# A convolution by spectra with a soft mixture of experts: a new order inside a step, and the filter's spectrum loaded two steps ahead

## The chip, the cores and the metric

The kernel runs on one core of one Trainium2 chip. The metric is device time in microseconds of one execution; lower is better. Engines are named as the profile does: PE (TensorE), with its weight loads as PEld, DVE (VectorE), ACT (ScalarE), POOL (GpSimd) and SP (SyncE, which here only issues transfers).

## What is computed

```python
def _attn_ref(x, h):                      # x (8, 5696, 128), h (5696, 128), float32
    B, S, D = x.shape
    L = 2 * S
    Xf = np.fft.rfft(x, n=L, axis=1)
    Hf = np.fft.rfft(h, n=L, axis=0)
    return np.fft.irfft(Xf * Hf[None], n=L, axis=1)[:, :S, :]

def _moe_ref(x, phi, w1, w2):             # x: the (45568, 128) rows of the above
    logits = x @ phi                      # 32 slots, 8 experts
    d = np.exp(logits - logits.max(0, keepdims=True))
    d /= d.sum(0, keepdims=True) + 1e-09
    slot_input = (d.T @ x).reshape(E, S_per_e, D)
    for e in range(E):
        slot_out[e] = np.maximum(slot_input[e] @ w1[e], 0.0) @ w2[e]
    c = np.exp(logits - logits.max(1, keepdims=True))
    c /= c.sum(1, keepdims=True) + 1e-09
    return c @ slot_out.reshape(n_slots, D)
```

A long convolution of 8 sequences with one filter, then a softmax over tokens (down each column of the logits) that gathers 32 slots, a small two-layer network on them, and a softmax over slots (along each row) that spreads them back.

## The kernel before

Both transforms of the convolution are products with constant tables on PE. The length is split as 90 x 64. The filter `h` goes first as block 0, then the 8 sequences; each block is 8 chunks. A loop over t = 0 to 79 (line 598) is a software pipeline written out by hand: every engine runs its instructions in the order in which the code records them. In one step:

- `stage_a` (t < 72): 128 small products of the folded input `xf` with the table `s1` (L245), in four tiles ("banks") of PSUM, each copied to `ft` by ACT (L251). `next_x` then folds the next input on POOL (L230) and issues loads.
- `stage_b1` (from t = 8, twice a step): forward products into `bt` (L285), then DVE multiplies them with the filter's spectrum `ht` (L309) and combines them into `yf` (L319). `ht` is made in steps 8 to 15, stored to `h_spec`, and from then on loaded a chunk at a time (`load_h`, L272); there are two `ht` buffers and two of each `yf`.
- `stage_b2`, one step later: backward products of `yf` (L335), copied by ACT to `zst` (L340) and stored to the tensor `z` (L343).
- From t = 26 on the rest works on a "pair" of chunks, spread over several steps. `pair(lag)` is the number of the pair whose turn is `lag` steps after its first; pairs start in even steps. `stage_c1` (even, lag 0) turns `z`, loaded to `zc`, into tokens `y`: two pairs of products (L388), folds on DVE (L393, L394), then four folds on POOL (L407). `stage_c2` (odd, lag 1) transposes `y` in four tiles (L416), copied by ACT to `yt` (L418). `stage_c3` (odd) gives the logits (L425), copied to `lt` (L428). `column_max` takes the running maximum of each column on DVE (L436, L441, L444). `stage_c4` (even, lag 2) transposes the logits (L454), takes the exponent of the column softmax into `dt` on ACT (L460) and the maximum of each row on DVE (L469), subtracted on POOL (L470). `stage_c5` (even) transposes `dt` (L477) into `d`. `softmax` finishes the row softmax: Exp on ACT (L485), token sums on DVE (L487 to L489), product on POOL (L490). `dispatch` multiplies `d` with `y` on PE (L501), and DVE adds the result to `acc` (L506). `stage_c6` (odd, lag 5) transposes the row softmax (L525) and stores it.

All PSUM tiles but `bt` come from one ring of four banks (`bank()`). A tile that gets a bank again waits until the engine that reads the last tile in it has done so: `yt`, `zst` and `ft` copies by ACT, the c1 folds and the addition to `acc` by DVE.

Steps 72 to 79 have no `stage_a`. After the loop come the stages of the last pairs, the network on the slots, and the product that writes the output.

Of the kernel before, what the change touches and what calls it, by code (L numbers as in the profile page):

```python
# [10 lines left out]
F32 = mybir.dt.float32  # L11
# [63 lines left out]
def kernel(  # L75
# [25 lines left out]
    P = 128  # L101
    B, S, D = x.shape
    NSL = moe_phi.shape[1]
    E, _, F = moe_w1.shape
# [5 lines left out]
    NJ = HALF // CH  # L110
    NU = (NP + 1) // 2
    KG = 2 * ((NU + NJ - 1) // NJ)
# [48 lines left out]
    bpool = front.enter_context(tc.tile_pool(name="bpool", bufs=1))  # L161
# [91 lines left out]
    prods, hs = {}, {}  # L253
# [8 lines left out]

    def spectrum(c):
        if c not in hs:
            hs[c] = bpool.tile([P, 2, KG * D], F32, name="ht", tag="ht", bufs=2)
            if c == NJ - 1:
                nc.gpsimd.memset(hs[c][:, :, :], 0.0)
        return hs[c]

    def load_h(c):  # L270
        if NJ <= c < (B + 1) * NJ:
            nc.sync.dma_start(out=spectrum(c)[:, :, :], in_=hd[c % NJ])  # L272
# [4 lines left out]
    def stage_b1(u):  # L277
        g, j, part, us = parts(u)
        bt = bps.tile([P, 2, 2, 2 * D], F32, name="bt", tag=f"bt{part}")
        for o, (i, n) in enumerate(us):  # L280
            for a in range(2):
                r = slice(a * HP, (a + 1) * HP)
                for q in range(n):
                    f_ = 2 * ((2 * i + q) % KG)
                    nc.tensor.matmul(bt[q * HP:(q + 1) * HP, a, o, :], wt[r, 2 * i + q, :],  # L285
                                     block(ft, g, r, j)[:, :, f_:f_ + 2, :].rearrange(
                                         "p s c d -> p c s d"),
                                     start=True, stop=True)
        m, r = len(us), slice(0, us[0][1] * HP)

        if m == 2:
            pv = bt[r, :, :, :].rearrange("p a o (c d) -> p (a o) c d", c=2)
        else:
            pv = bt[r, :, 0, :].rearrange("p a (c d) -> p a c d", c=2)
        k = 2 * m
        pi = bpool.tile([P, 4, 2, D], F32, name="p", tag="pi", bufs=1)
        ht = spectrum(u // 2)
        h0 = part * (KG - 2) * D
        hv = [ht[r, v, h0:h0 + k * D].rearrange("p (k d) -> p k d", d=D) for v in range(2)]
        for v, p_ in ((1, pi[r, 0:k, :, :]), (0, pv)):  # L300
            if g:
                h_ = hv[v]
            else:
                i = us[0][0]
                h_ = turn[r, v, :, i:i + m].unsqueeze(3).broadcast_to([r.stop, 2, m, D]) if m == 2 else \
                    turn[r, v, :, i].unsqueeze(2).broadcast_to([r.stop, k, D])
            if g or m == 1:
                h_ = h_.unsqueeze(2).broadcast_to([r.stop, k, 2, D])
                nc.vector.tensor_tensor(out=p_, in0=pv, in1=h_, op=AL.mult)  # L309
            else:  # L310
                for a in range(2):
                    nc.vector.tensor_tensor(
                        out=p_[:, 2 * a:2 * a + 2, :, :], in0=pv[:, 2 * a:2 * a + 2],
                        in1=h_[:, a].unsqueeze(2).broadcast_to([r.stop, m, 2, D]), op=AL.mult)
        if g:
            y_ = bpool.tile([P, 4 - 2 * part, 2, D], F32, name="yf", tag=f"yf{part}", bufs=2)
            prods[u] = y_
        for c, op_ in ((0, AL.subtract if g else AL.add), (1, AL.add if g else AL.subtract)):
            nc.vector.tensor_tensor(out=y_[r, 0:k, c, :] if g else hv[c], in0=pv[:, :, c, :],  # L319
                                    in1=pi[r, 0:k, 1 - c, :], op=op_)  # L320

    def stage_b2(u):
        g, j, part, us = parts(u)
        if g == 0:
            return
        m = len(us)
        y_ = prods.pop(u)
        n = us[0][1]
        st = bpool.tile([P, 2 - part, 2, 2 * D], F32, name="zst", tag=f"zst{part}", bufs=2 - part)
        bz = [bank() for _ in range(n)]  # L330
        for o, (i, _) in enumerate(us):
            for q in range(n):
                r = slice(q * HP, (q + 1) * HP)
                for a in range(2):
                    nc.tensor.matmul(bz[q][a * HP:(a + 1) * HP, o * 2 * D:(o + 1) * 2 * D],  # L335
                                     vt[r, i, a, :],
                                     y_[r, a * m + o, :, :].rearrange("p c d -> p (c d)"),
                                     start=True, stop=True)
        for q in range(n):
            nc.scalar.activation(st[:, 0:m, q, :],  # L340
                                 bz[q][:, 0:m * 2 * D].rearrange("p (o x) -> p o x", o=m), AF.Copy)
        k, q0 = m * n, 2 * us[0][0]
        nc.sync.dma_start(  # L343
            out=zd[g - 1][q0:q0 + k, :, :, :].rearrange("q r c d -> r q (c d)"),
            in_=st[:, :, :, :].rearrange("p o q x -> p (o q) x")[:, 0:k, :])
# [66 lines left out]
    def stage_c2(T):  # L412
        for k in (3, 1, 0, 2) if tail else (3, 2, 1, 0):
            p = bank()
            for i in range(CH):
                nc.tensor.transpose(p[:, i * TR:(i + 1) * TR], ys[T][0:TR, k * CH + i, 0:D],  # L416
                                    ident[0:TR, 0:TR])
            nc.scalar.activation(yt[:, k * CH:(k + 1) * CH, :, :], of_tokens(p), AF.Copy)  # L418
# [75 lines left out]
    def dispatch(T):  # L494
        ap_ = bank()
        d_ = ds.pop(T)
        y_ = ys.pop(T)
        for i in range(CH):
            for k in range(Q):
                r = slice(k * NSL, (k + 1) * NSL)  # L500
                nc.tensor.matmul(ap_[r, 0:D + 1], d_[:, i, r], y_[:, k * CH + i, :],  # L501
                                 start=(i == 0), stop=(i == CH - 1))
        if T == 0:
            nc.vector.tensor_copy(out=acc[:, :], in_=ap_[:, 0:D + 1])
        else:
            nc.vector.scalar_tensor_tensor(out=acc[:, :], in0=acc[:, :],  # L506
                                           scalar=scales.pop(T)[:, 0:1], in1=ap_[:, 0:D + 1],
                                           op0=AL.mult, op1=AL.add)
# [89 lines left out]
    for t in range(last_front + 1):  # L598
        us = [2 * (t - LAG_B) + k for k in range(2)] if t >= LAG_B else []

        def pair(lag):
            T, half = divmod(t - LAG_C - lag, 2)
            return T if half == 0 and 0 <= T < NT else None

        for u in us:
            stage_b1(u)
        if us:
            c = us[0] // 2
            if c < NJ:
                store_h(c)  # L610
            else:
                del hs[c]
            load_h(c + 1)
        for u in wait_b2:
            stage_b2(u)
        wait_b2 = us
        if t < NA:
            stage_a(t)
            next_x(t + NJ)
        if pair(3) is not None:  # L620
            dispatch(pair(3))
        T, U = pair(0), pair(2)
        if t == last_front:
            assert T is None and U is None
            stage_c2(pair(1))
            for u in us:
                stage_b2(u)
            wait_b2 = []
            V = pair(1)
            stage_c6(V - 2)  # L630
            stage_c3(V)
            column_max(V)
            break
        rows = (lambda: None) if U is None else (lambda: stage_c4(U))
        after = None
        if T is not None:
            after = stage_c1(T, rows)
        else:
            rows()
        if pair(1) is not None:  # L640
            stage_c2(pair(1))
        if pair(5) is not None:
            stage_c6(pair(5))
        if after:
            after()
        if pair(-2) is not None:
            load_pair(pair(-2))
        if U is not None:
            stage_c5(U)
        if pair(1) is not None:  # L650
            stage_c3(pair(1))
        if pair(1) is not None:
            column_max(pair(1))
        if U is not None:
            softmax(U)
        if t == NA:
            lead.close()
            wts = inner.enter_context(tc.tile_pool(name="wts", bufs=1, side="right"))
            w1s = wts.tile([P, E, F], F32, name="w1s")
        if NA <= t < NA + E:  # L660
            nc.sync.dma_start(out=w1s[:, t - NA, :], in_=moe_w1[t - NA])

    T = V + 1
    (_, n0, p0), (_, n1, p1) = z_blocks(N1)
# [213 lines left out]
```

## Time and profile before

| | |
|---|---|
| median of 3 runs | 973.12 us (970.54 to 976.52) |
| the profiled execution | 971.23 us, its span 969.1 us |
| PE, PEld busy | 778.9 us (80%), 524.8 us (54%) |
| DVE, ACT, POOL busy | 678.4 us (70%), 468.9 us (48%), 367.8 us (38%) |
| mean granted clock of PE | 0.92 |
| moved by DMA | 223.94 MB, mean 231 GB/s |

A row of a group or of the timeline names the line of the kernel, the engine, the operation, what it writes and reads, and the shapes; "idle before <-releaser" is the time the engine stood still just before, and what ended it. A row of the waits has the total in us, how many times, and the longest. "issue" as a releaser means that the profile shows nothing that the engine waited for. PEclk is the share of its full clock that PE was granted. Each float32 product stands as two matrix instructions.

### The profile page before, as it was taken

How to read it: one execution, taken by the hardware profiler on the slowest of the kernel's cores; microseconds unless marked ns; L12 is line 12 of the kernel's file. 1: busy time of each engine (PE TensorE's matmuls, PEld its weight loads, DVE VectorE, ACT ScalarE, POOL GpSimd, SP SyncE). 2: the span in 40 equal slices, each digit the busy share in tenths (PEclk: the TensorE clock that was granted, in tenths of full speed). 3: DMA queues.
4: the chain of work that ended last, by engine and by line, in shares of the span. 5: the costliest groups of instructions: out<-in, count | busy, mean ns of one | idle time of the engine just before them, and what ended most of it. 6: DMA issues, size and time to landing. Idle time of an engine off the chain costs nothing.

```text
span 969.1 us, 36172 instructions
## 1 busy us (share of the span) xinstructions
PE 778.9 (80%) x15860; PEld 524.8 (54%) x15860; DVE 678.4 (70%) x1117; ACT 468.9 (48%) x1040; POOL 367.8 (38%) x357
## 2 busy tenths in 40 slices
PE   2677678779879898888888988998978888786893
PEld 2655455545555565565555655655655443244783
DVE  5378677657758778687776777877868997673542
ACT  1432244335545565455555555555645454465442
POOL 1024333344444444445554554543314224463000
PEclk9999899979989999999998999999989998887955
DMA  9642678886757777686777776766748988853598
GB/s 220 208 130 114 209 228 261 284 256 219 240 182 253 236 239 234 207 260 217 230 232 229 231 236 221 233 213 210 223 162 287 307 287 223 240 187 125 223 405 339
DMA packets 95783, 223.94 MB, mean 231 GB/s; under 512 B 7382, under 2 KB 57046, under 8 KB 92485
## 3 DMA queue, kind: packets, MB, share of 16 engines
q1 hardware_dynamic: 95051, 221.29, 70.8%
q8 instruction: 124, 2.03, 0.9%
q10 hardware_dynamic: 576, 0.36, 0.2%
q14 instruction: 32, 0.26, 0.1%
HBM read 140.10 MB, written 81.42 MB: 229 GB/s over the span
## 4 chain that ended last, share of the span: by engine, by line
PE 49%; DMA 12%; DVE 11%; issue 6%; ACT 5%; POOL 3%; SPq 0%; DVEq 0%; ACTq 0%; POOLq 0%
PE bank L245 12%; PE bank L388 10%; PE bt L285 7%; PE bank L335 5%; PE bank L416 4%; DMA out_dram<-o 3%; DVE yf L319 3%; DMA zd<-z 3%; ACT zst L340 3%; PE bank L425 3%; DVE p L309 3%; DVE bt L309 2%; DMA z<-zst 2%; PE bank L501 2%; DMA cl<-c_t 2%
## 5 line engine op out<-in xcount | busy, mean ns | idle before, releaser
L245 PE MATMUL bank<-s,xf 128*32 128x90 f32 (+1 forms) x9216 | 210.5, 249 | 62.7 <-issue 25.2
L245 PEld LDWEIGHTS bank<-s,xf 128*32 128x32 f32 x9216 | 193.4, 138 | 96.2 <-ACT zst L340 41.6
L230 POOL TENSOR_TENSOR xf<-xc 128x512 f32<-128x512 f32 x100 | 125.5, 1276 | 253.2 <-PE bank L245 246.6
L251 ACT ACTIVATE ft<-bank 128x384 f32<-128x384 f32 x288 | 140.6, 492 | 116.3 <-PE bank L245 96.6
L340 ACT ACTIVATE zst<-bank 128x256 f32<-128x256 f32 (+1 forms) x248 | 100.4, 485 | 124.4 <-PE bank L335 107.6
L309 DVE TENSOR_TENSOR p<-bt,ht 128x512 f32<-128x512 f32 (+2 forms) x128 | 116.7, 912 | 35.7 <-DMA ht<-h_spec 26.4
L285 PE MATMUL bt<-ft,wt 64*64 64x256 f32 x1620 | 118.1, 408 | 27.5 <-DVE yf L319 13.3
L319 DVE TENSOR_TENSOR yf<-bt,p 128x256 f32<-128x256 f32 (+2 forms) x256 | 126.5, 535 | 4.4
L388 PE MATMUL bank<-zc,i 128*64 128x512 f32 x480 | 117.7, 613 | 4.1 <-DMA z<-zst 1.9
L309 DVE TENSOR_TENSOR bt<-bt,ht 128x512 f32<-128x512 f32 (+2 forms) x128 | 118.0, 922 | 0.0
L436 DVE TENSOR_REDUCE mx<-lt 64x1 f32<-64x360 f32 x64 | 33.1, 518 | 99.9 <-ACT lt L428 99.4
L335 PE MATMUL bank<-yf,vt 64*64 64x256 f32 x1440 | 98.5, 380 | 5.1 <-DVE om L394 3.6
L285 PEld LDWEIGHTS bt<-ft,wt 64*64 64x64 f32 x1620 | 58.5, 141 | 80.6 <-issue 44.0
L418 ACT ACTIVATE yt<-bank 128x360 f32<-128x360 f32 x128 | 54.9, 472 | 80.6 <-PE bank L416 80.6
L416 PE MATMUL bank<-ident,y 109*128 109x109 f32 x512 | 69.4, 290 | 24.6 <-DVE acc L506 10.8
L407 POOL TENSOR_TENSOR y<-y,op 128x512 f32<-128x512 f32 x64 | 77.5, 1210 | 9.9 <-DVE op L393 7.1
L416 PEld LDWEIGHTS bank<-ident,y 109*128 109x128 f32 x512 | 58.0, 159 | 35.6 <-issue 16.9
L335 PEld LDWEIGHTS bank<-yf,vt 64*64 64x64 f32 x1440 | 58.7, 134 | 31.3 <-DVE om L394 5.4
L407 POOL TENSOR_TENSOR y<-y,om 128x512 f32<-128x512 f32 x54 | 64.7, 1198 | 2.1
L462 POOL MEMSET dt<- 64x8 f32 x32 | 3.4, 107 | 145.7 <-issue 111.0
L501 PE MATMUL bank<-y,d 128*32 128x129 f32 x1024 | 38.7, 283 | 24.3 <-issue 21.0
L388 PEld LDWEIGHTS bank<-zc,i 128*64 128x64 f32 x480 | 29.9, 138 | 51.6 <-issue 43.7
(104 smaller groups left out, 899.1 us busy)
## 6 DMA issues: line engine op xcount, KB each, us to landing
ht<-h_spec SPq DMA_DIRECT2D x64, 768.0 KB
zc<-z SPq DMA_DIRECT2D x30, 1024.0 KB
z<-zst SPq DMA_DIRECT2D x56, 512.0 KB
xc<-in_x_dram SPq DMA_DIRECT2D x52, 320.0 KB
z<-zst SPq DMA_DIRECT2D x64, 256.0 KB
out_dram<-o SPq DMA_DIRECT2D x16, 1024.0 KB
zc<-z SPq DMA_DIRECT2D x30, 416.0 KB
h_spec<-ht SPq DMA_DIRECT2D x8, 768.0 KB
```

The source lines that it names most:

```text
L230: eng.tensor_tensor(out=to, in0=ab[0], in1=ab[1], op=AL.subtract if comp else AL.add)
L245: nc.tensor.matmul(p[r:r + HALF, k * W:k * W + w_], x_, s1[:, comp, a, 0:w_], start=True, stop=True)
L251: nc.scalar.activation(to, v, AF.Copy)
L285: nc.tensor.matmul(bt[q * HP:(q + 1) * HP, a, o, :], wt[r, 2 * i + q, :], block(ft, g, r, j)[:, :, f_:f_ + 2, :].rearrange("p s c d -> p c ...
L309: nc.vector.tensor_tensor(out=p_, in0=pv, in1=h_, op=AL.mult)
L319: nc.vector.tensor_tensor(out=y_[r, 0:k, c, :] if g else hv[c], in0=pv[:, :, c, :], in1=pi[r, 0:k, 1 - c, :], op=op_)
L335: nc.tensor.matmul(bz[q][a * HP:(a + 1) * HP, o * 2 * D:(o + 1) * 2 * D], vt[r, i, a, :], y_[r, a * m + o, :, :].rearrange("p c d -> p (c ...
L340: nc.scalar.activation(st[:, 0:m, q, :], bz[q][:, 0:m * 2 * D].rearrange("p (o x) -> p o x", o=m), AF.Copy)
L388: nc.tensor.matmul(p[h_ * HP:(h_ + 1) * HP, :], i1[0:kr, tab, :], t_[0:kr, h_, o, :, q, :], start=True, stop=True)
L407: eng.tensor_tensor(out=part_, in0=part(v, 0), in1=o_[:, :, :], op=sign)
L416: nc.tensor.transpose(p[:, i * TR:(i + 1) * TR], ys[T][0:TR, k * CH + i, 0:D], ident[0:TR, 0:TR])
L501: nc.tensor.matmul(ap_[r, 0:D + 1], d_[:, i, r], y_[:, k * CH + i, :], start=(i == 0), stop=(i == CH - 1))
```

## The change

It touches the `ht` and `yf` buffers and the order of the loop's body. `ht` gets a third buffer, and each `yf` loses one. The spectrum for step t + 2 is loaded in step t (in step 15 those for 16 and 17), behind the `z` stores on SP. The two halves of `stage_b1` and of the last step's `stage_b2` alternate. In an odd step `stage_c2` and `stage_c6` now precede `stage_a`. `dispatch` moves from the odd step with lag 3, behind `stage_a`, to the even step with lag 4, ahead of it. `column_max` moves from the end of the odd step to the next even step, behind `dispatch` and `stage_a` in the order of recording and ahead of `stage_c1`. `softmax` moves from the end of the even step to the end of the next odd one, behind `stage_c3`. The arithmetic and the number of instructions that compute are the same.

```diff
--- before.py
+++ after.py
@@ -262,7 +262,7 @@
 
     def spectrum(c):
         if c not in hs:
-            hs[c] = bpool.tile([P, 2, KG * D], F32, name="ht", tag="ht", bufs=2)
+            hs[c] = bpool.tile([P, 2, KG * D], F32, name="ht", tag="ht", bufs=3)
             if c == NJ - 1:
                 nc.gpsimd.memset(hs[c][:, :, :], 0.0)
         return hs[c]
@@ -313,7 +313,7 @@
                         out=p_[:, 2 * a:2 * a + 2, :, :], in0=pv[:, 2 * a:2 * a + 2],
                         in1=h_[:, a].unsqueeze(2).broadcast_to([r.stop, m, 2, D]), op=AL.mult)
         if g:
-            y_ = bpool.tile([P, 4 - 2 * part, 2, D], F32, name="yf", tag=f"yf{part}", bufs=2)
+            y_ = bpool.tile([P, 4 - 2 * part, 2, D], F32, name="yf", tag=f"yf{part}", bufs=1)
             prods[u] = y_
         for c, op_ in ((0, AL.subtract if g else AL.add), (1, AL.add if g else AL.subtract)):
             nc.vector.tensor_tensor(out=y_[r, 0:k, c, :] if g else hv[c], in0=pv[:, :, c, :],
@@ -602,65 +602,58 @@
             T, half = divmod(t - LAG_C - lag, 2)
             return T if half == 0 and 0 <= T < NT else None
 
-        for u in us:
-            stage_b1(u)
+        for k in range(2):
+            if us:
+                stage_b1(us[k])
+            if wait_b2:
+                stage_b2(wait_b2.pop(0))
         if us:
             c = us[0] // 2
             if c < NJ:
                 store_h(c)
             else:
                 del hs[c]
-            load_h(c + 1)
-        for u in wait_b2:
-            stage_b2(u)
+            for n in (c + 1, c + 2) if c == NJ - 1 else (c + 2,):
+                if c >= NJ - 1:
+                    load_h(n)
         wait_b2 = us
+        T, U, V = pair(0), pair(2), pair(1)
+        if V is not None:
+            stage_c2(V)
+            if t == last_front:
+                while wait_b2:
+                    stage_b2(wait_b2.pop(0))
+            if pair(5) is not None:
+                stage_c6(pair(5))
+        if pair(4) is not None:
+            dispatch(pair(4))
         if t < NA:
             stage_a(t)
             next_x(t + NJ)
-        if pair(3) is not None:
-            dispatch(pair(3))
-        T, U = pair(0), pair(2)
-        if t == last_front:
-            assert T is None and U is None
-            stage_c2(pair(1))
-            for u in us:
-                stage_b2(u)
-            wait_b2 = []
-            V = pair(1)
-            stage_c6(V - 2)
-            stage_c3(V)
-            column_max(V)
-            break
-        rows = (lambda: None) if U is None else (lambda: stage_c4(U))
-        after = None
+        if U is not None:
+            column_max(U)
         if T is not None:
-            after = stage_c1(T, rows)
-        else:
-            rows()
-        if pair(1) is not None:
-            stage_c2(pair(1))
-        if pair(5) is not None:
-            stage_c6(pair(5))
-        if after:
+            after = stage_c1(T, (lambda: None) if U is None else (lambda: stage_c4(U)))
             after()
+        elif U is not None:
+            stage_c4(U)
         if pair(-2) is not None:
             load_pair(pair(-2))
         if U is not None:
             stage_c5(U)
-        if pair(1) is not None:
-            stage_c3(pair(1))
-        if pair(1) is not None:
-            column_max(pair(1))
-        if U is not None:
-            softmax(U)
+        if V is not None:
+            stage_c3(V)
+            if pair(3) is not None:
+                softmax(pair(3))
         if t == NA:
             lead.close()
             wts = inner.enter_context(tc.tile_pool(name="wts", bufs=1, side="right"))
             w1s = wts.tile([P, E, F], F32, name="w1s")
-        if NA <= t < NA + E:
+        if NA <= t < last_front:
             nc.sync.dma_start(out=w1s[:, t - NA, :], in_=moe_w1[t - NA])
-
-
+        if t == last_front:
+            column_max(V)
+            dispatch(V - 1)
 
     T = V + 1
     (_, n0, p0), (_, n1, p1) = z_blocks(N1)
```

## The prediction

> **What bounds the kernel now.** I read the page's busy times first, then the chain of waits for the length of a step, then TensorE's waits in the steady stretch, then the timeline of one pair of steps, and last the granted clock around a long TensorE idle.
>
> ```profile
> PE 778.9 (80%) x15860; PEld 524.8 (54%) x15860; DVE 678.4 (70%) x1117; ACT 468.9 (48%) x1040; POOL 367.8 (38%) x357
> PEclk9999899979989999999998999999989998887955
> ```
>
> No engine is full over the span, but PE and DVE are the two that matter. The chain of waits gives the steady pair: step 30 begins (its first `bt` product) at 238.67 and step 72 at 733.38, so 21 pairs of an even and an odd step take (733.38 - 238.67) / 21 = 23.56 us each.
>
> ```profile
> 238.67 1.46 PE bt L285 x24
> ...
> 733.38 1.46 PE bt L285 x24
> ```
>
> TensorE's waits between 238 and 733 us:
>
> ```profile
> PE bank L501 <- issue: 21.0, 6, 4.3
> PE bank L416 <- DVE acc L506: 10.8, 7, 2.0
> PE bank L245 <- ACT zst L340: 9.4, 37, 0.3
> PE bank L416 <- issue: 8.3, 3, 3.6
> PE bank L245 <- issue: 5.8, 7, 1.6
> ```
>
> "issue" is idle time for which the profile names no releaser: with two small rows it is 36.9 us here, 1.76 a pair. One pair in the timeline (start, duration, engine, line, tile):
>
> ```profile
> 595.11 1.07 PEld L285 LDWEIGHTS bt<-ft,wt 64*64 64x64 f32 x24 [0.59 <-issue]
> ...
> 595.30 0.48 ACT L428 ACTIVATE lt<-bank 128x360 f32<-128x360 f32 x1 [0.50 <-PE bank L425]
> ...
> 606.37 0.62 ACT L485 ACTIVATE L<-L 128x512 f32<-128x512 f32 x1
> ...
> 607.03 0.69 DVE L487 TENSOR_REDUCE rs<-L 128x16 f32<-128x512 f32 x1 [0.24 <-ACT L L485]
> ...
> 608.83 1.16 DVE L309 TENSOR_TENSOR p<-bt,ht 128x1024 f32<-128x1024 f32 x1
> ...
> 611.42 1.07 PE L501 MATMUL bank<-y,d 128*32 128x129 f32 x32
> ...
> 614.55 0.34 DVE L506 SCALAR_TENSOR_TENSOR acc<-acc,dn,bank 128x129 f32<-128x129 f32 x1
> 615.01 0.39 PEld L416 LDWEIGHTS bank<-ident,y 109*128 109x128 f32 x4 [1.46 <-POOL xf L230]
> 615.04 0.56 PE L416 MATMUL bank<-ident,y 109*128 109x109 f32 x4 [1.28 <-DVE acc L506]
> ```
>
> The even step is 595.11 to 605.77 (10.66), the odd one to 616.91 (11.14): 21.80, and the 1.76 of "issue" makes the mean 23.56. What the reader should see is `acc`: dispatch ended at 612.49, yet L506, which empties its bank, ran at 614.55, because it stands in DVE's queue behind the products of the spectrum (608.83 onward). TensorE paid for it at the fourth `c2` tile, which reuses that bank.
>
> ```profile
> 587.00:590.00 3.00, 0.00 (x0) 0.00 (x0) 2.26 (x5) 0.00 (x0) 2.25 (x2) 1.00 0.97 342
> 590.50:593.90 3.40, 3.40 (x23) 3.27 (x19) 0.35 (x1) 1.47 (x4) 0.00 (x0) 0.50 0.53 163
> 279.90:283.30 3.40, 0.00 (x0) 0.00 (x0) 2.17 (x5) 0.00 (x0) 2.17 (x2) 1.00 0.98 350
> 283.30:290.10 6.80, 6.48 (x45) 4.49 (x48) 0.35 (x1) 2.71 (x6) 0.00 (x0) 0.50 0.32 101
> ```
>
> The number before the last two is the clock: after 3 us without a matmul TensorE runs at 0.50 for 3.4 us, after 3.4 us once for 6.8 us.
>
> **What the Trainium skill says.** TensorE: Matmul & The Clock Gate, section "What's actually happening", says that an idle window of about 3.4 us halves the clock until a busy one; the windows above agree (0.50). The same page, section "Architectural detail: the array is 16× 32×32, not 1× 128×128", calls ScalarE and VectorE strict FIFO; `acc`, ready at 612.49 and run at 614.55, agrees.
>
> **The change part by part.** I lay out the new pair by hand from start to start of the rows above; 0 is the first `bt` product of an even step, right behind `c3`.
>
> *Backward between forward products.* Same instructions: b1 1.13 (595.11 to 596.24) and b2 1.23, now in pieces 0.75, 0.82, 0.38, 0.41, done at 2.36. The 0.71 that `a` waited for the first `zst` copy mostly goes: that copy starts 0.47 after b2's first part, at 2.04, lasts 0.60, so the next bank is had at 2.71, a wait of 0.35. In the odd step a wait of POOL's hides it.
>
> *Softmax later, column maximum later.* The odd step now ends c3, `lt` copy, Exp L485, row sums, and only then come the even step's products in DVE's queue. `lt` starts at 0.19 and ends at 0.67, Exp 0.62 ends at about 1.32, L487 to L489 take 1.80 (607.03 to 608.83), so products start at 3.17. Before, they started at 597.17 - 595.11 = 2.06, behind the column maximum (1.35, 595.82 to 597.17). That maximum now stands behind `acc`, where DVE otherwise waits for c1: nothing while c1 is late, up to 1.35 if it is not. The Exp fits before `zst` needs ACT.
>
> *Dispatch in the even step, ahead of `a`.* It runs from 2.71 to 3.79 (1.08). Its bank is freed by `acc`, in DVE's queue behind all products: products plus `acc` took 608.83 to 614.89 = 6.06, so `acc` ends at 3.17 + 6.06 = 9.23 and TensorE goes on at 9.35 (0.12 later, as 614.89 to 615.01). The built order of the changed kernel shows whom that stops: in 12 of 20 such steps the second of the four `a` tiles waits for L506, in 5 the third, in 3 the first c1 product. They would be ready at 3.79 + 0.63 = 4.42, at 5.05 and at 6.30. The wait is 4.93, 4.30 or 3.05, mean 4.5 us. Queued behind it are the rest of `a`, c1 (whose folds DVE and POOL await) and the next odd step. Before, the same `acc` was due only after `a` and dispatch, and cost 10.8 us in all. The even step: 3.79 + 2.50 (`a`) + 4.5 + 4.91 (c1, L454, L477: 600.86 to 605.77) = 15.7.
>
> *c2 and c6 at the odd step's head.* c1's second half ends at 15.1, `op` starts 0.19 later, POOL's four folds 0.77 after that, at 16.07, and take 606.14 to 611.03 = 4.89, to 20.96. c2's last tile follows to 21.35, c6 0.42, `a` 2.50, c3 0.75: 25.05. So the odd step is 9.35 against 11.14. It is rid of dispatch and of its old waits (0.71, 1.46, 0.39), and waits about 1.7 for POOL. The row softmax's product L490 moves behind the odd step's x fold on POOL, which is 38% busy and idle there.
>
> The pair is 25.05 before "issue" and clock. Of "issue" I keep 0.7 of 1.76: it sat in the run of `a`, dispatch and c2, which is now broken by a long wait in which anything late arrives (0 to 1.76). For the clock I add 1.7: an idle of 4.5 us is longer than the 3.0 above, and 3.4 us at 0.50 lose 1.7 us of work (0 to 3.4, two windows as at 283.3). Sum 27.45, so +3.9 a pair, times 21 = +82 us.
>
> *Spectrum two steps ahead, three buffers.* Between 100 and 215 us DVE waits 25.8 us, 8 times, for `ht`; the first, 8.5, stays, as that load is issued in the same step. The other 17.3 can go, but DMA is 81% busy from 120 to 210, and the load now stands behind two z stores and ahead of the x loads on SP's queue: between 0 and -17, I take -8. In the steady stretch these waits were nothing already. One `yf` buffer costs nothing: the write waits for b2's part, over at 1.57, and comes at 3.17 + 2.33; without that cover a fraction of a us a step.
>
> *Steps 72 to 79 without `a`.* Two pairs took 779.64 - 740.60 in the chain of waits, 19.52 each. With the new order the second c1 product waits for `acc`: 9.35 + 3.39 (the rest of c1), 0.19 + 0.77 to POOL's first fold, 4.89 for the four, 0.36 + 0.42 + 0.75 for c2's last tile, c6 and c3 give 20.1, with the clock's 1.7 21.8: +2.3 x 4 = +9 us. The rest, from 812 us on, is unchanged.
>
> Total 82 - 8 + 9 = +83. The profiled execution was 971.2 us (span 969.1), so 1054; it lay 1.9 below the median of 973.1, so about 1055 against the median.
>
> **The rivals.**
> - *The wait stands, the clock does not fall.* For it: 5 us idles are new here, and shorter idles of about 3 us (at 469 us) passed. Against: the windows shown. The pair is 25.75, +2.2 x 21 = 46, less 8, plus 4: about 1015.
> - *Two half-clock windows each time*, as after 283 us: another 1.7 x 21 + 7 = 43: about 1098.
> - *Other side: the bank does not bind.* If L506 were done when the second `a` tile wants its bank, the pair would be 25.05 - 4.5 + 1.76 = 22.3, -1.25 x 21 = -26, with the ramp's -8 about 939. It decides at the place of L506: a mean wait under 34 / 21 = 1.6 us, `acc` over by about 6 us into the even step, is not slower. For it: the odd step's shortening is real. Against: eight products, 5.72 us from 608.83 to 614.55, stand ahead of L506 in DVE's order.
>
> **How the numbers follow.** The wait with one clock window 0.65; without clock loss 0.15; with two windows 0.13; the bank does not bind 0.07. The likeliest gives 1055, by itself 1035 to 1075. The range 1005 to 1098 takes in the second and most of the third. About 1% is what a measurement of this kernel tells from no change: faster 0.05, same 0.02, slower 0.93.
>
> **What would show it.** A large wait of PE bank L245 for DVE acc L506, about 4 to 5 us, some 17 times, and 3 of L388 for the same; PEclk lower in the slices from 240 to 740 us; L416 waiting for POOL y; even steps near 16 to 18 us, odd ones near 9.5; DVE idle before L487 for Exp; the `ht` waits shrunk to the first. It is wrong if L506 runs before the products, or if even steps stay under 12 us.

## The result and the profile after

The changed kernel takes 1041.82 us (median of 4 runs, 1041.10 to 1043.86), the kernel before 974.36 (4 runs): a ratio of 1.070, 95% interval 1.066 to 1.074. The profiled execution was 1041.1 us with a span of 1039.0, so the span grew by 69.9. The prediction said +83.

Busy times and clock record of the page, after:

```profile
PE 808.7 (78%) x15860; PEld 544.2 (52%) x15860; DVE 659.8 (64%) x1117; ACT 471.3 (45%) x1040; POOL 368.9 (36%) x357
PEclk9999899999988989998999988899999897797965
```

The work is the same (15860 products), yet PE is busy 29.8 us longer than before (808.7 against 778.9). A lower clock does most of that: by the clock record, PE was busy at half speed for 171.7 us of the whole execution, before for 119.4, and half of the difference is 26. DVE is busy 18.6 us less; more on this at the end. TensorE's waits in the steady stretch, 233 to 794.3 us (total, times, longest):

```profile
PE bank L245 <- DVE acc L506: 60.7, 17, 4.2
PE bank L416 <- POOL y L407: 21.1, 42, 0.7
PE bank L245 <- issue: 5.6, 6, 2.1
PE bank L388 <- DVE acc L506: 4.7, 3, 2.2
PE bank L245 <- DVE acc L504: 4.1, 1, 4.1
```

The wait of 10.8 us for `acc` at `c2` is gone, and one of 60.7 us has come at `a`, 17 times 3.6 us. One even step in the timeline:

```profile
615.47 1.09 PE L285 MATMUL bt<-ft,wt 64*64 64x256 f32 x16
...
616.69 0.69 DVE L487 TENSOR_REDUCE rs<-L 128x16 f32<-128x512 f32 x1 [3.51 <-ACT L L485]
617.41 0.17 DVE L488 TENSOR_SCALAR rs<-rs 128x16 f32<-128x16 f32 x1
617.62 0.25 DVE L489 RECIPROCAL rs<-rs 128x16 f32<-128x16 f32 x1
617.79 1.16 DVE L309 TENSOR_TENSOR p<-bt,ht 128x1024 f32<-128x1024 f32 x1
...
618.70 1.09 PE L501 MATMUL bank<-y,d 128*32 128x129 f32 x32
...
623.66 0.34 DVE L506 SCALAR_TENSOR_TENSOR acc<-acc,dn,bank 128x129 f32<-128x129 f32 x1
624.05 3.55 PEld L245 LDWEIGHTS bank<-s,xf 128*32 128x32 f32 x96 [3.81 <-DVE acc L506]
624.05 3.89 PE L245 MATMUL bank<-s,xf 128*32 128x90 f32 x96 [3.63 <-DVE acc L506]
```

Dispatch L501 is done at 619.8, but L506, behind the products that began at 617.79, ends at 624.00, and 0.05 later the second `a` tile starts. The 96 weight loads of this and the two following tiles then take 3.55 us. The table by windows (the number before the last two is the clock) shows why: half speed follows the idle. The last row is the whole steady stretch.

```profile
615.47:633.71 18.24, 14.61 (x236) 9.05 (x232) 10.56 (x20) 7.01 (x16) 6.40 (x7) 0.81 0.47 151
624.00:628.00 4.00, 3.95 (x98) 3.67 (x100) 1.26 (x4) 0.98 (x2) 0.00 (x0) 0.50 0.25 101
670.90:686.50 15.60, 11.89 (x236) 7.15 (x232) 10.54 (x20) 7.00 (x16) 6.45 (x7) 1.00 0.49 156
233.00:794.30 561.30, 456.98 (x9008) 303.85 (x9008) 352.56 (x609) 272.26 (x604) 232.03 (x217) 0.93 0.62 199
```

The step from 670.90 is an even step whose clock did not fall: its second `a` tile waited nearly as long for L506 (3.51 us against 3.63), yet it took 15.60 us instead of 18.24.

Step 30 starts at 232.97 and step 72 at 795.35, so a pair takes (795.35 - 232.97) / 21 = 26.78 us, 16.57 even and 10.21 odd; before it was 23.56, 11.02 and 12.53. The 69.9 us are 3.22 x 21 = +67.7 in the steady pairs, -5.7 up to step 30 and +7.9 after step 72.

### The profile page after: what moved, and what is told of

Read it like the earlier page. It is cut to its first block, busy times and chain, and to the rows that moved or that the text cites. A ratio compares the mean times of both kernels' runs of the same rounds, so it can differ in the third digit from the quotient of the medians.

```text
span 1039.0 us, 36277 instructions
## 1 busy us (share of the span) xinstructions
PE 808.7 (78%) x15860; PEld 544.2 (52%) x15860; DVE 659.8 (64%) x1117; ACT 471.3 (45%) x1040; POOL 368.9 (36%) x357
## 4 chain that ended last, share of the span: by engine, by line
PE 29%; DVE 21%; POOL 14%; DMA 9%; issue 5%; ACT 2%; DVEq 0%; SPq 0%; POOLq 0%; ACTq 0%
POOL y L407 12%; PE bank L245 12%; PE bank L388 8%; DVE yf L319 5%; DVE p L309 5%; DVE bt L309 4%; DMA out_dram<-o 3%; DMA zd<-z 2%; POOL L L470 2%; PE bank L425 2%; PE bank L416 2%; DMA z<-zst 2%; DVE y L393 2%; DVE rm L469 2%; DVE rs L487 1%
## 5 line engine op out<-in xcount | busy, mean ns | idle before, releaser
L245 PE MATMUL bank<-s,xf 128*32 128x90 f32 (+1 forms) x9216 | 235.4, 263 | 118.2 <-DVE acc L506 60.7
L245 PEld LDWEIGHTS bank<-s,xf 128*32 128x32 f32 x9216 | 215.2, 143 | 135.3 <-DVE acc L506 63.9
L388 PE MATMUL bank<-zc,i 128*64 128x512 f32 x480 | 134.5, 686 | 16.2 <-DVE acc L506 15.8
L285 PE MATMUL bt<-ft,wt 64*64 64x256 f32 x1620 | 126.5, 399 | 19.5 <-DVE ht L319 9.8
L335 PE MATMUL bank<-yf,vt 64*64 64x256 f32 x1440 | 114.4, 394 | 2.7 <-issue 2.7
L487 DVE TENSOR_REDUCE rs<-L 128x16 f32<-128x512 f32 x32 | 21.9, 684 | 118.6 <-ACT L L485 118.6
L285 PEld LDWEIGHTS bt<-ft,wt 64*64 64x64 f32 x1620 | 59.1, 136 | 64.9 <-issue 35.9
L407 POOL TENSOR_TENSOR y<-y,op 128x512 f32<-128x512 f32 x64 | 77.5, 1211 | 11.6 <-DVE op L393 8.7
L393 DVE TENSOR_TENSOR y<-bank,y 128x512 f32<-128x512 f32 x32 | 22.1, 691 | 92.1 <-PE bank L388 91.8
L416 PEld LDWEIGHTS bank<-ident,y 109*128 109x128 f32 x512 | 51.5, 144 | 55.1 <-POOL y L407 42.0
L335 PEld LDWEIGHTS bank<-yf,vt 64*64 64x64 f32 x1440 | 62.5, 140 | 29.4 <-issue 8.1
L388 PEld LDWEIGHTS bank<-zc,i 128*64 128x64 f32 x480 | 33.6, 159 | 76.0 <-issue 42.9
L407 POOL TENSOR_TENSOR y<-y,om 128x512 f32<-128x512 f32 x54 | 64.0, 1185 | 2.1
L490 POOL TENSOR_TENSOR L<-L,rs 128x512 f32<-128x512 f32 x32 | 33.6, 1049 | 77.2 <-PE bt L285 38.2
```

Of the source, the lines that this page charges most:

```text
L245: nc.tensor.matmul(p[r:r + HALF, k * W:k * W + w_], x_, s1[:, comp, a, 0:w_], start=True, stop=True)
L388: nc.tensor.matmul(p[h_ * HP:(h_ + 1) * HP, :], i1[0:kr, tab, :], t_[0:kr, h_, o, :, q, :], start=True, stop=True)
L407: eng.tensor_tensor(out=part_, in0=part(v, 0), in1=o_[:, :, :], op=sign)
```

## The experiments

Ratios are against the kernel before on the same chip, with 95% intervals. "Pair" is worked out as above, from the starts of steps 30 and 72.

### Where the dispatch and the softmax stand

**disp_odd**: the dispatch goes back to the odd step.

```diff
-        if pair(4) is not None:
-            dispatch(pair(4))
         if t < NA:
             stage_a(t)
             next_x(t + NJ)
+        if pair(3) is not None:
+            dispatch(pair(3))
...
-            dispatch(V - 1)
```

> The changed kernel with dispatch put back into the odd step, behind stage_a, three steps after the pair's first (all else as changed). Theory (the loss is the bank that dispatch holds until L506, which stands behind the products): the wait of L245 for L506 goes, with it the half clock; a pair has no long wait on TensorE but DVE runs row sums, products and column maximum in a row ahead of the c1 folds, about 22.3 plus 1 us, against 26.7 changed and 23.6 before: about 960 us. Rival (the row sums ahead of the products, or POOL ahead of c2, are the loss): stays above 1020.

**disp_head**: the dispatch is recorded first in its even step, so that L506 stands ahead of the products on VectorE.

```diff
+        if pair(4) is not None:
+            dispatch(pair(4))
         for k in range(2):
             if us:
                 stage_b1(us[k])
...
-        if pair(4) is not None:
-            dispatch(pair(4))
```

> The changed kernel with dispatch still in the even step and ahead of stage_a, but recorded at the step's very start, so that L506 stands ahead of the products in DVE's queue. Theory: the bank is free by about 3 us, the wait goes; a pair about 22.3 us: about 940 us. Rival (dispatch in the even step ahead of stage_a is itself the loss, wherever L506 stands): above 1020.

**soft_even**: the row softmax goes back to the end of the even step.

```diff
         if U is not None:
             stage_c5(U)
+            softmax(U)
...
-            if pair(3) is not None:
-                softmax(pair(3))
```

> The changed kernel with the row softmax (Exp, sums, product) put back to the end of the even step. Theory: the even step's products start about 1.2 us earlier, so the wait for L506 falls from 3.8 to about 2.5 us: 21 pairs by 1.2 is 25 us, about 1015 us; the rest of the loss stays. Rival (the row sums are the cause): the whole loss goes, 975 us or less.

Measured: disp_odd 981.72 us (1.0044, 1.0008 to 1.0079; pair 24.39), disp_head 964.37 (0.9843, 0.9769 to 0.9918; pair 23.58), soft_even 1007.29 (1.0237, 1.0133 to 1.0341; pair 25.02). In the first two the wait at L245 is gone, as the theory said, but both came some 20 us short of the gain expected. TensorE's largest wait in the steady stretch, first of disp_odd, then of disp_head, is that of `c2` for GpSimd's folds:

```profile
PE bank L416 <- POOL y L407: 41.6, 71, 0.7
```

```profile
PE bank L416 <- POOL y L407: 40.2, 67, 0.7
```

It was 21.1 us in the changed kernel. There VectorE, done with its products and the column maximum, waited for TensorE's late `c1` products and folded them at once, so that GpSimd's first fold starts 0.37 us into the odd step (median of the 21 pairs). In disp_odd and disp_head VectorE reaches these folds later, and GpSimd starts at 1.71 and 1.70. The expected 22.3 us a pair (one more for disp_odd) had the early start in it.

It also had nothing for the clock, and these short waits bring half speed too. In one odd step of disp_odd (TensorE's rows, then two windows):

```profile
247.39 0.59 PE L416 MATMUL bank<-ident,y 109*128 109x109 f32 x4 [0.67 <-POOL y L407]
248.53 0.59 PE L416 MATMUL bank<-ident,y 109*128 109x109 f32 x4 [0.55 <-POOL y L407]
249.79 0.59 PE L416 MATMUL bank<-ident,y 109*128 109x109 f32 x4 [0.67 <-POOL y L407]
```

```profile
246.70:249.80 3.10, 1.22 (x10) 0.79 (x9) 2.45 (x6) 1.48 (x4) 2.95 (x3) 1.00 0.90 276
250.60:253.90 3.30, 3.30 (x86) 3.12 (x88) 0.00 (x0) 1.62 (x4) 0.00 (x0) 0.50 0.99 385
```

All 15 times that the clock falls in its steady stretch, two or three such waits end in the 3.6 us before or reach into its start. TensorE is busy at half speed there for 64.9 us, in disp_head's for 47.3; half of that is lost, 1.55 and 1.13 us a pair.

soft_even agrees with the theory: products start earlier, the 17 waits for L506 shrink to 43.9 us in all (2.6 each), the clock falls less often (33.9 us of busy TensorE at half speed, where the changed kernel has 73.7), and the rest stays.

### Which part brings the wait

**b_disp**: the kernel before, with the dispatch alone moved to the even step.

```diff
+        if pair(4) is not None:
+            dispatch(pair(4))
         if t < NA:
             stage_a(t)
             next_x(t + NJ)
-        if pair(3) is not None:
-            dispatch(pair(3))
...
+            dispatch(V - 1)
```

> The kernel before with one part of the change alone: the dispatch of a pair moved from the odd step to the following even step, ahead of the column transform (lag 4). Theory (the accumulation L506 stands behind the four products of the step on VectorE, and the bank that it frees is the one TensorE asks for next): a wait of L245 or L388 on L506 of 3 to 4 us in each of the 21 pairs, and the clock falls after it; some 1005 to 1025 us against about 975. Rival (the bank is not what TensorE waits for, the row softmax at the step's head makes the loss): within 1% of the kernel before.

It took 969.56 us: 0.9894 (0.9821 to 0.9966), pair 23.59. The theory as I had put it is wrong: with L506 as late as ever the move alone costs nothing. In the built program, b_disp gives the dispatch's bank to the second half of c1, eight or nine tiles later; the changed kernel gives it to the second or third `a` tile. The ring has four banks, and which tile inherits which of them is settled when the program is built. The part of the change that turns this touches no bank.

**bd_spec**: b_disp and the spectrum two steps ahead.

```diff
-            load_h(c + 1)
+            for n in (c + 1, c + 2) if c == NJ - 1 else (c + 2,):
+                if c >= NJ - 1:
+                    load_h(n)
```

with `ht` of three buffers and `yf` of one, as in the change.

> b_disp with the spectrum loaded two steps ahead (three ht buffers, one yf). TensorE and VectorE keep b_disp's order of instructions; the dispatch's bank falls to the second or third column-transform tile in 17 steps, as in the changed kernel, where in b_disp it fell to the second half of c1, eight tiles later. Theory: a wait of L245 on acc L506 of 3 to 4 us in most pairs, and the clock behind it: 1015 to 1060 us against 970 for b_disp. Rival (the bank decides nothing): 960 to 975.

**no_spec**: the changed kernel, with that edit and the number of `ht` buffers undone.

> The changed kernel with the spectrum loaded one step ahead again (two buffers of ht; all else stays). Each engine but SyncE has the same instructions in the same order as in the changed kernel; but in the built program the four PSUM banks fall otherwise: of the 20 dispatches with a next column transform, 14 have a bank that nobody asks for before L506 is long over, and 6 the bank of a c1 product, where in the changed kernel 17 have that of the second or third column-transform tile. Theory (it is the tile that inherits the dispatch's bank that decides, not where the dispatch stands): L245's 64.8 us on acc go, 940 to 975 us. Rival 1 (VectorE's order makes the even step long whatever the bank): 1030 to 1055. Rival 2 (the spectrum two steps ahead is what helps): slower than the changed kernel.

**own_bank**: the changed kernel, with a bank for the dispatch alone.

```diff
-    rings = [mid.enter_context(tc.tile_pool(name="ps", bufs=4, space=PSUM))]
+    rings = [mid.enter_context(tc.tile_pool(name="ps", bufs=3, space=PSUM))]
+    psd = mid.enter_context(tc.tile_pool(name="psd", bufs=1, space=PSUM))
...
-        ap_ = bank()
+        ap_ = psd.tile([P, 512], F32, name="bank", tag="bank")
```

> The changed kernel with a PSUM bank for the dispatch alone and three in turn for all else; the order of instructions on each engine is the same. Theory: nothing of the column transform waits for L506 any more; three banks in turn cost some tenths of a us at the ACT copies: 950 to 1000 us. Rival (VectorE's late products set the step): 1030 to 1055.

Measured: bd_spec 1028.19 us (1.0521, 1.0409 to 1.0634; pair 25.69), no_spec 977.98 (1.0091, 1.0062 to 1.0119; pair 23.82), own_bank 956.25 (0.9816, 0.9735 to 0.9898; pair 23.46). The list of who waited for `acc` over the whole execution (total, times; its first rows) puts the four side by side. The changed kernel:

```profile
  PEld bank L245: 68.1, 18
  PE bank L245: 64.7, 18
```

b_disp, where nothing at L245 waits:

```profile
  PEld bank L388: 2.8, 4
```

bd_spec, the same order of products and of VectorE's work with other banks:

```profile
  PEld bank L245: 64.4, 18
  PE bank L245: 61.0, 18
```

no_spec, where only the reading of `acc` at the very end is left:

```profile
  PEld bank L753: 1.3, 1
```

So the wait is made by two things together: `acc` is late, and a tile that TensorE needs soon inherits its bank. Neither alone brings it: b_disp and no_spec have the late `acc` with another heir, disp_head has an early `acc`. Each is within 2% of the kernel before. no_spec missed its range by 3 us: there too GpSimd's first fold starts late (1.71 us into the odd step), `c2` waits for the folds (37.0 us in the steady stretch), and TensorE is busy at half speed for 60.1 us, a loss of 1.43 a pair. own_bank takes the wait from the changed kernel without touching its order, and is 1.8% faster than the kernel before with one bank fewer in turn. Why the load's place turns the choice of banks stays open.

### What the idle costs by the clock

**warm_wait**: in dispatch steps the first `a` tile is computed six times, to keep TensorE busy in the wait.

```diff
-            for k in range(CH):
+            for k in [k for _ in range(1 + (again if m == 0 else 0)) for k in range(CH)]:
...
-            stage_a(t)
+            stage_a(t, 5 if pair(4) is not None else 0)
```

> The changed kernel, with the first of the four tiles of stage_a multiplied five times over again in the steps that dispatch (the same numbers into the same bank, 3.1 us of added matmuls), so that TensorE works through most of its wait for L506. Theory (the halved clock after the wait costs about 1.2 us a pair): PEclk near 1.00 and 15 to 25 us faster than changed, about 1020 us, though 2.7 us of work was added to each such step. Rival (the clock costs nothing there): 1040 us or more.

**warm_big**: seven products of 128x384 ahead of that tile, which then overwrites them.

```diff
+            for _ in range(warm if m == 0 else 0):
+                nc.tensor.matmul(p[:, 0:384], ident[:, :],
+                                 s1[:, :, :, :].rearrange("p k a c -> p (k a c)")[:, 0:384],
+                                 start=True, stop=True)
...
-            stage_a(t)
+            stage_a(t, 7 if pair(4) is not None else 0)
```

> The changed kernel with seven products of 128x384 of no use (identity by the table s1, into the first column-transform bank, which the true products then overwrite) ahead of the column transform in each step with a dispatch, so that TensorE works while the accumulation is awaited; only 7 instructions more, against 320 in warm_wait. Theory (the idle wait costs a second time, by the clock that falls after it): the wait for L506 shrinks to under 1 us, its place is filled, the record in the steady stretch stays at 0.96 or more, and the time falls by 1.2 us in each of 21 pairs: some 1015 to 1020. Rival 1 (the fallen clock costs nothing, since VectorE sets the step): 1037 to 1045. Rival 2 (the fill is longer than the wait): 1050 or more.

warm_wait missed: 1070.32 us (1.0904, 1.0813 to 1.0994). Its waits for L506 are gone, but idle time without a releaser has come in their place:

```profile
PE bank L245 <- issue: 58.3, 38, 3.1
```

That run settles nothing about the clock. warm_big says more, though it too fell outside its ranges. It took 1033.11 us (1.0564, 1.0508 to 1.0620), pair 26.28. Its steady stretch by windows, and the added products in the groups by line:

```profile
230.80:781.50 550.70, 519.86 (x9302) 332.71 (x9302) 352.19 (x609) 272.69 (x604) 232.25 (x217) 1.00 0.62 203
```

```profile
L238 PE MATMUL bank<-s,ident 128*128 128x384 f32 x294 | 100.4, 493 | 0.0
```

The clock is 1.00 instead of 0.93, and no wait for L506 is left. But the fill takes 100.4 / 21 = 4.78 us a pair where the wait was (60.7 + 4.7 + 4.1) / 21 = 3.31. In the changed kernel's steady stretch the clock record has 81.9 us at half speed, with TensorE busy in 73.7 of them; half of that is 36.9, or 1.76 a pair (before: 38.1 busy, 0.91 a pair). The clock falls 19 times, 16 of them around or just behind one of the 18 waits of L245 for `acc`; the two without a fall were 2.39 and 3.51 us long, so the length alone does not decide it. The sum 26.78 - 3.31 + 4.78 - 1.76 = 26.5 meets the 26.28 measured. The second price of the wait is real; it came out at 1033 rather than 1015 to 1020 because my fill was 1.5 us too long.

### The spectrum alone, and one small VectorE instruction

**b_spectrum**: the kernel before with the edit of bd_spec alone.

> The kernel before with the spectrum alone loaded two steps ahead (three buffers of ht, one of yf). Theory: the seven waits of L309 on the spectrum of 3 to 8 us in the ramp go, and nothing is lost to the single buffer of yf: 5 to 8 us faster, some 967 to 970. Rival: the load is hidden anyway, or the single buffer of yf takes it back (L319 waiting for L335 a pair of times a step): within 3 us, or up to 15 us slower.

It took 975.65 us: 1.0009 (0.9973 to 1.0045), pair 23.57. VectorE's waits between 100 and 215 us:

```profile
DVE p L309 <- PE bt L285: 19.0, 8, 7.8
DVE p L309 <- DMA ht<-h_spec: 7.3, 1, 7.3
```

So the rival holds. The seven waits for the spectrum did go (before, 25.8 us in 8 waits), and nearly all of their time is now a wait of the same line for `bt`: in the ramp the products wait for TensorE as well.

**b_no_eps**: the kernel before without L488, as the expectation says.

> The kernel before without L488, the addition of 1e-9 to the row sums (left out; the sums are 1 or more). Theory: L488 takes 0.87 to 1.03 us there because it waits for a running fold L407 of GpSimd, against 0.17 where GpSimd is idle, so the products of the odd step start up to 1 us earlier: 5 to 15 us faster. Rival: the reciprocal L489 takes the wait over, or the start of the products binds nothing: within 4 us.

It took 973.08 us: 0.9984 (0.9950 to 1.0018), pair 23.43. The rival holds, and not because the reciprocal takes the wait over (it lasts 0.25 us there, as before): the instruction costs VectorE up to 1 us a pair and the kernel nothing.

### A version that beats both

**c2_late**: disp_head with `c2` and `c6` behind the column transform, as before the change.

```diff
+        if t < NA:
+            stage_a(t)
+            next_x(t + NJ)
         if V is not None:
             stage_c2(V)
...
-        if t < NA:
-            stage_a(t)
-            next_x(t + NJ)
```

> disp_head with the transposes of the folded output (L416, stage_c2 and c6) put back behind the column transform of the odd step, as in the kernel before. Theory: the 43 to 48 us of L416 waiting for GpSimd's folds L407 there go, as the folds end while TensorE works on the column transform; 20 to 40 us faster than disp_head, some 930 to 945. Rival: the wait moves to the products of c3 and column maximum behind it and the odd step stays at 13 us: 955 to 970.

It took 898.55 us: 0.9191 (0.9134 to 0.9248), faster than its range, pair 20.43. Its steady stretch by windows, and the wait that bound disp_head there:

```profile
227.00:656.10 429.10, 415.41 (x9031) 282.42 (x9026) 346.87 (x609) 273.10 (x605) 229.74 (x215) 1.00 0.80 261
```

```profile
PE bank L416 <- POOL y L407: 0.2, 1, 0.2
```

The 40.2 us have become 0.2, PE is busy 415.4 of 429.1 us (97%), and the clock stays at 1.00. That second effect is why it passed the expectation: disp_head had its stretch at 0.95, and the waits removed gave back their clock too. TensorE was busy at half speed for 47.3 us there and is for 3.4 here; half of the difference, 22.0, and the 40.0 of the waits make 62 of the 66 us between the two stretches (495.3 and 429.1). Which of the change's remaining parts this version still needs was not tried.

## Why the prediction was right, and where it was not

*The wait at the bank* was right: L245 for L506 17 times, L388 3 times, as the built order said. Its size was over: predicted 4.5 us a pair, measured 3.31. In the step shown the second `a` tile waited 3.63 against 4.93. Two terms make that up. `acc` ended at 8.53 into the step, not 9.23, and the tile could start at 4.95 (620.42), not 4.42, as dispatch began at 3.23, not 2.71. Over 21 pairs that is 25 us too much.

*The mis-sized term in VectorE's chain* is "L487 to L489 take 1.80": it took 1.10. The products started at 2.32, not 3.17. I had carried over L488 from a place where it shared its time with GpSimd.

*The clock*: 1.7 a pair predicted, 1.76 measured. But the kernel before already lost 0.91 a pair in this way, and the prediction's account of it, 21.80 and 1.76 of "issue", has no term for that: the pair it took the 21.80 from ran at full clock and had a wait of 1.28 for `acc` where the mean is 10.8 / 21 = 0.51. So of the growth by 3.22 a pair the clock is 0.85 and the wait for `acc` 2.80; the rest, -0.43, is what the other terms leave. Its rule for the fall was also too narrow: the second idle that it shows was 3.78 us long (279.84 to 283.62), not 3.4, and disp_odd has the clock fall after idles of 0.55 to 0.67. So a stretch of 3.4 us without any work, as it cites it, is not needed for a fall.

*"Issue"*: 0.7 predicted, 13.7 us / 21 = 0.65 measured. So the even step is 15.7 - 1.19 + 1.76 and half of 0.65, 16.6; it was 16.57.

*The odd step* was 9.35 predicted, 9.48 in the pair shown (605.99 to 615.47) and 10.21 in the mean, so 0.5 under the mean with its share of "issue". That error and the one of the wait have opposite signs, and 11 of the 25 us cancel. The pair: 27.45 - 1.19 + 0.5 = 26.8, as measured.

*The ramp*: -8 predicted, -5.7 measured, and that looks better than it was. The step "the other 17.3 can go" failed: they went and came back as a wait for `bt`, and b_spectrum starts its step 30 at 241.47, no earlier than the kernel before (238.60). no_spec, without the early load, starts it at 234.79. Most of the gain is thus the rest of the new order's.

*Steps 72 and on*: +9 predicted, +7.9 measured.

*The cause* was named too simply. The prediction charged the wait to "dispatch in the even step, ahead of `a`" and put the spectrum down as a small gain. The dispatch alone, in the kernel before, costs nothing, and the changed kernel without the early spectrum is some 60 us faster than with it (1.009 against 1.070 of the kernel before). The forecast held because the heir of the bank was read from the built program of the whole change; the same numbers would have been wrong for the dispatch alone.

*The rivals.* "The clock does not fall" is ruled out by the windows and warm_big. "Two windows each time" happens in the step shown (half speed from 623 to 629.8), yet others have one or none: 81.9 us at half speed are some 24 windows of 3.4 us in 21 pairs. "The bank does not bind" is what no_spec is: the prediction priced it at 939, 22.3 a pair, and it measured 978, 23.82 a pair. The price left out the clock (1.43 a pair) and that VectorE, no longer kept waiting, would let GpSimd start its folds 1.34 us later (1.71 against 0.37); and it kept 1.76 of "issue" where no_spec has 9.4 / 21 = 0.45. The three make 23.8.

## What to carry to other kernels

When an accumulator's bank is emptied late, ask which tile inherits the bank, and read it from the built program after every change, also one that only moves a load: here the same order of products cost 59 us more with other heirs (b_disp and bd_spec). A wait of TensorE can be paid twice, by its length and by the half speed behind it: in the changed kernel 16 of 18 waits of 2.4 to 4.2 us, in disp_odd and disp_head also two or three waits of 0.55 to 0.67 us close together. Likewise removing such waits can pay twice, once no other wait takes their place. Give the late engine the slack first: putting the transposes behind independent work took off some 65 us (disp_head 0.984 of the kernel before, c2_late 0.919).

## What the runs showed of the hardware

L488 adds a constant to 128x16 numbers. Its durations (shortest, median, longest, in ns), in the kernel before:

```profile
L488 DVE TENSOR_SCALAR rs<-rs x32: 174/874/1030, 229.5 to 889.7; 128x16 f32<-128x16 f32 x32
```

and in the changed kernel:

```profile
L488 DVE TENSOR_SCALAR rs<-rs x32: 174/175/178, 234.9 to 959.5; 128x16 f32<-128x16 f32 x32
```

In the kernel before, each of the 26 long ones ends some 0.03 us after a fold L407 of GpSimd that was running when it was due. In the changed kernel no L407 runs there; L488 meets no instruction of GpSimd, or only the last 0.15 us of one, and takes 0.17 us either way. The Trainium skill, page SBUF — State Buffer, section "Who interferes with whom", says that `tensor_scalar` can take the port pair that VectorE shares with GpSimd, and that whoever comes second waits for the whole instruction of the other; these durations agree. The busy time of VectorE counts such a wait as work: L488 is 24.8 us of it before and 5.6 after, which is all of the 18.6 us that VectorE was busy less. No run here moved GpSimd's instruction alone.

warm_wait's 58.3 us of "issue" came with 3360 more products in TensorE's stream (19220 instead of 15860) and as many weight loads, while warm_big's 294 brought almost none. The Trainium skill, page Runtime: NRT & Kernel Launch, section "Instruction fetch mechanics", says that instructions are streamed in blocks of 256 at a cost that is mostly hidden. Whether these idles are such blocks arriving late is not shown by any run. What the run shows is 58.3 us of idle TensorE, in 21 pairs, for which no data and no bank is named, where the changed kernel has 5.6 at that line.
